# A fused attention and routing kernel: the third chunk's projections, the first DMAs and the order of the opening

## Chip, cores, metric

The kernel runs on one core of a Trainium2 chip. The metric is the device time of one execution in microseconds, the median over nine runs. Each core has TensorE (PE), VectorE (DVE), ScalarE (ACT), GpSimd (POOL) and SyncE (SP), all with instruction queues of their own, and 16 DMA engines that they share.

## What is computed

Attention with sketched features for 4 batches of 4 heads, 1088 positions of 32 numbers; its output, as 4352 rows of 128, is the input of 8 experts, weighted by 8 rounds of row and column scaling. S1 and S2 have 8 rows of 32; they come as 64-bit floats.

```python
def phi(x):
    a = np.einsum('rd,bhsd->bhsr', S1, x)
    b = np.einsum('rd,bhsd->bhsr', S2, x)
    return np.einsum('bhsi,bhsj->bhsij', a, b).reshape(*x.shape[:-1], r * r)
q_p, k_p = (phi(q), phi(k))
kv = np.einsum('bhsf,bhsd->bhfd', k_p, v)
z = np.sum(k_p, axis=2)
num = np.einsum('bhsf,bhfd->bhsd', q_p, kv)
den = np.einsum('bhsf,bhf->bhs', q_p, z)[..., None] + 1e-06
attn = num / den

x = np.ascontiguousarray(attn.transpose(0, 2, 1, 3)).reshape(B * S, H * D)
logits = x @ w_gate
P = np.exp(logits - logits.max())
for _ in range(8):
    P /= P.sum(1, keepdims=True) + 1e-09
    P /= P.sum(0, keepdims=True) + 1e-09
    P *= N / E
for e in range(E):
    out += P[:, e:e + 1] * (np.maximum(x @ w1[e], 0.0) @ w2[e])
```

## The kernel before

**Stages.** The opening computes batch 0's attention by itself. Then the experts' matmuls begin on what is ready of batch 0, with experts 0 and 1 unweighted, and the attention of batches 1 to 3 and the routing are woven in between their steps. From then on the experts 1 to 7 work on inputs weighted by the routing. The generator `steps()` (L1121) yields one step of expert work at a time: a matmul pair of the first layer (`first`, L920, matmul at L926, relu on ScalarE at L930) and, some steps later, pairs of the second layer (`into`, L1092, matmul at L1111). `fill(n)` (L1186) runs steps until n units of them are used, and carries the rest over. For groups of two tiles a unit is about two steps of 256 columns.

**Order.** Inside `manual_schedule` blocks TensorE and VectorE, in the first block ScalarE too, take the order of the program; elsewhere a planner may move instructions. `keep_in_program_order` holds a single instruction in place. Each engine runs its queue in order, so an instruction that waits holds up those behind it. SyncE issues most DMAs and waits in its queue too.

**The opening.** S1 is loaded by SyncE and S2 by ScalarE into one tile `raw`, each broadcast over the partitions (L101, L102). SyncE then loads keys, a first part of the queries and the values of batch 0, queries of batch 1, the rest of batch 0's queries, the gate's weights, expert 0's weights, and keys and values of batch 1 (L181 to L185, L292 to L295). 14 matmuls on ones (L114) run in the meantime. `projections()` (L258) turns 64-bit floats into 32-bit ones on VectorE (L34 to L46), transposes them (`st`, L262) and makes `wd` (L263), the projections of each head in its own partitions. `repeated()` (L267) makes on GpSimd, from `st`, `wq` (two heads in 64 partitions), `wdq` and `wz` (L280: one head in its partitions, zeros in the others). Then come the turned keys (`transpose_k`, L307, L309), their projections (`keys_ab`, L319, L324, copied out by ScalarE), their products on VectorE (`keys_products`, L336) and sums over positions (`keys_sums`, L352). ScalarE copies these to `kvz` (`keys_kept`, L367).

**Queries of batch 0** go in three chunks of positions, 0 to 512, 512 to 800 and 800 to 1088. `query_products(c)` projects them, ScalarE copies one factor to `ph` (L391), and `multiply` (L396, VectorE) multiplies it by the other, which stays in PSUM. `fractions(c, m)` (L404) makes numerators (m = 0) and denominators (m = 1), and `divide(c)` (L407 to L422, VectorE) writes `xT`, the experts' input. In `query_products` the chunks 0 and 1 use row tiles: two matmuls of 64 input partitions and 128 output columns run side by side (L381). Chunk 2 uses column tiles with all 128 input partitions and the weights `wz` (L387), one pair of heads at a time, in four groups of two.

**PSUM.** `bank()` gives one of four rotating banks; the others carry the tags s0 to s3, used by `query_products` of chunks 0 and 1, by `fractions` of chunks 1 and 2 (s2, s3) and by the experts' sums (`DIRECT` group: s0, s1).

**Batch 1's queries** go another way: `transpose_q(1)` (L302), `queries_ab(1)` (L438, copied by ScalarE at L441), then through DRAM (`qa`, `qb`, stored by SyncE and GpSimd, L445 and L449; read back by `repeat_a` and `repeat_b`, L455 and L458).

**Expert steps.** `step(c)` of `two` (L938) takes the four combinations of two blocks f of hidden units and two tiles t of positions in the order f = c // 2, t = c % 2 (L939, L940), so a block's second step already needs the second tile.

**Weights for three-tile groups.** `sums_of_four` (L226) makes 16 sums of weight blocks on GpSimd (L242) and stores them to DRAM by SyncE (L246) for later groups. `weigh` (L690) multiplies inputs by routing weights on GpSimd. `weigh_kept` (L706, called at L1148) weights the kept outputs of the early experts, one block into an expert at q = 0.

Of the kernel before, what the change touches and what calls it, by code (L numbers as in the profile page):

```python
# [50 lines left out]
def kernel(  # L51
# [12 lines left out]
    nc = tc.nc  # L64
# [29 lines left out]
    def bank():  # L94
        return aps.tile([P, 512], F32, tag="a", name="a")
# [2 lines left out]

    words = mybir.dt.size(S1.dtype) // 4
    raw = consts.tile([P, 2, words * D], U32, name="raw")  # L100
    for n, (s, queue) in enumerate(((S1, nc.sync), (S2, nc.scalar))):  # L101
        queue.dma_start(out=raw[:, n], in_=s.bitcast(U32).unsqueeze(0).to_broadcast([P // R, R, words * D]))  # L102

    def starts(tile_, c0, blocks):

# [120 lines left out]
    def sums_of_four(e, w2):  # L226

        ws = pools[0].tile([P, len(FORMS), FO // 4, H2], F32, tag="ws4", name="ws4")
        if e in stored_four:
            nc.sync.dma_start(out=ws, in_=stored_four[e])  # L230
            return ws

        def blocks(bs):
            b = w2[:, bs[0][1]::4, H2 * bs[0][0]:H2 * (bs[0][0] + 1)].unsqueeze(1)
            if len(bs) == 1:
                return b
            step = (bs[1][1] - bs[0][1]) * DM + (bs[1][0] - bs[0][0]) * H2
            return AP(tensor=b.tensor, offset=b.offset, ap=[b.ap[0], [step, 2], *b.ap[2:]])

        c = 0  # L240
        for ns, x, y, off in FOURS:
            tc.keep_in_program_order(nc.gpsimd.tensor_tensor(ws[:, c:c + len(ns)], blocks(x), blocks(y),  # L242
                                                             op=Alu.subtract if off else Alu.add))
            c += len(ns)
        stored_four[e] = dram.tile([P, len(FORMS), FO // 4, H2], F32, name=f"ws4{e}")
        nc.sync.dma_start(out=stored_four[e], in_=ws)  # L246
        return ws

    wd = consts.tile([P, 2, H, R], F32, name="wd")
    wq = consts.tile([P, 2, 2, R, R], F32, name="wq")

    wz = wk.tile([P, H, W9], F32, tag="xt", name="xt", bufs=1).rearrange("p h n -> p (h n)")[:, 0:2 * H * R * R]
    wz = wz.rearrange("p (n h i j) -> p n h i j", n=2, h=H, i=R)
    wdq = consts.tile([P, 2, H * R], F32, name="wdq")

    def projections():  # L258
        flat = raw.rearrange("p n d -> p (n d)")
        s12 = f64_to_f32(nc, consts, flat, (P, 2 * D)) if words == 2 else flat.bitcast(F32)  # L260
        st = consts.tile([P, 2, 32], F32, name="st")
        nc.vector.transpose(out=st.rearrange("p n r -> p (n r)"), in_=s12)  # L262
        nc.vector.tensor_tensor(wd, st[:, :, 0:R].unsqueeze(2).to_broadcast([P, 2, H, R]),  # L263
                                own.unsqueeze(1).unsqueeze(3).to_broadcast([P, 2, H, R]), op=Alu.mult)
        return st

    def repeated(st):  # L267
        def repeat(out, column):
            one = column.unsqueeze(2).to_broadcast([P, R, R])
            nc.gpsimd.tensor_tensor(out[:, 0], st[:, 0, 0:R].unsqueeze(2).to_broadcast([P, R, R]), one, op=Alu.mult)  # L270
            nc.gpsimd.tensor_tensor(out[:, 1], st[:, 1, 0:R].unsqueeze(1).to_broadcast([P, R, R]), one, op=Alu.mult)

        for s in range(2):
            repeat(wq[:, :, s], half[:, s:s + 1])


        nc.gpsimd.tensor_copy(wdq[:, 0], wd[:, 0].rearrange("p h r -> p (h r)"))
        nc.gpsimd.tensor_copy(wdq[:, 1].rearrange("p (r h) -> p r h", h=H), wd[:, 1].rearrange("p h r -> p r h"))
        for h in range(H):
            repeat(wz[:, :, h], own[:, h:h + 1])  # L280

    wdf = wd.rearrange("p n h r -> p (n h r)")
    wqf = wq.rearrange("p n h i j -> p n (h i j)")
# [84 lines left out]

    chunks = ((0, 512), (512, 800), (800, S))

    def query_products(c, i=None):


        lo, hi = chunks[c]
        n = hi - lo
        if c < 2:
            banks = [[mps.tile([P, 512], F32, tag=f"s{2 * i + m}", name="s") for m in range(2)] for i in range(2)]
            for m in range(2):
                for i in range(2):
                    sl = slice(64 * i, 64 * (i + 1))  # L380
                    nc.tensor.matmul(banks[i][m][:, 0:n], wqf[sl, m, :], qT[sl, lo:hi], start=True, stop=True,  # L381
                                     tile_position=(64 * i, 0))
        else:
            banks = {i: [bank(), bank()]}
            for m in range(2):
                for s in range(2):
                    nc.tensor.matmul(banks[i][m][64 * s:64 * (s + 1), 0:n],  # L387
                                     wz[:, m, 2 * i + s].rearrange("p i j -> p (i j)"), qT[:, lo:hi],
                                     start=True, stop=True, tile_position=(0, 64 * s))
        for j in range(2) if c < 2 else (i,):  # L390
            nc.scalar.copy(phs[0][:, j, lo:hi], banks[j][0][:, 0:n])  # L391
            queries[0, c, j] = banks[j][1][:, 0:n]

    def multiply(c, i):
        lo, hi = chunks[c]
# [8 lines left out]
            nc.tensor.matmul(t[64 * i:64 * (i + 1), 0:n], kvz[:, m, i].rearrange("p h d -> p (h d)"),  # L404
                             phs[0][:, i, lo:hi], start=True, stop=True, tile_position=(0, 64 * i))

    def divide(c):  # L407


        lo, hi = chunks[c]  # L410
        n = hi - lo
        nb = n // 32
        pn, pd = (queries.pop((0, c, "pn", m)) for m in range(2))
        rd = wk.tile([P, 512], F32, tag="rd", name="rd")
        nc.vector.transpose(out=rd[:, 0:n], in_=pd[:, 0:n])
        rc = wk.tile([P, 16], F32, tag="rc", name="rc")[:, 0:nb]
        nc.vector.tensor_scalar_add(rc, rd[:, 0:n].rearrange("p (b r) -> p b r", r=32)[:, :, 0], 1e-6)
        nc.vector.reciprocal(rc, rc)
        rd = wk.tile([P, 512], F32, tag="rd", name="rd")
        nc.vector.transpose(out=rd[:, 0:n].rearrange("p (b r) -> p b r", r=32),  # L420
                            in_=rc.unsqueeze(2).to_broadcast([P, nb, 32]))
        nc.vector.tensor_tensor(xT[:, lo:hi], pn[:, 0:n], rd[:, 0:n], op=Alu.mult)  # L422

# [508 lines left out]
    def two(k):  # L932

        j, q = blocks[k]
        n = groups[items[j][0]][1]
        h, ts, (later_h, earlier_h, t13) = hs[k] = room_of(k)

        def step(c):  # L938
            f, t = 2 * q + c // 2, c % 2  # L939
            first(k, f, t * n, (t + 1) * n, h[c], k % 2)  # L940

        def less(out, a, b):
            nc.vector.tensor_tensor(out, a, b, op=Alu.subtract)  # L943
# [177 lines left out]
    def steps():  # L1121

        todo, sums_at, t = {}, {}, 0
        for k in range(len(blocks) + 5):
# [5 lines left out]
            if k < len(blocks):  # L1130
# [11 lines left out]
                if q == 1 and j + 1 < first_weighted and not direct_of(j + 1) and loaded_w[j + 1][2] is None:  # L1142
                    w1, w2, _ = loaded_w[j + 1]
                    w = w1, w2, sums_of_two(items[j + 1][1], w2)
                    loaded_w.update({i: w for i in loaded_w if items[i][1] == items[j + 1][1]})
                if q == 0:
                    if weighted and 1 <= es.index(e) <= es[0] + 1:
                        weigh_kept(g, es.index(e) - 1)  # L1148
                if k == len(blocks) - HELD:
                    kept_to_sums(g)  # L1150
                m, step, sums_ = (four if tiles == 3 else two)(k)
# [34 lines left out]
    def fill(n):  # L1186
        owed[0] += n
        while owed[0] > 0.25:
            owed[0] -= next(work)

    with tc.manual_schedule(engines={engines.DVE, engines.PE, engines.Activation}):
        st = projections()
        repeated(st)
        halves = ((0, NT // 2), (NT // 2, NT))
        transpose_k(0, halves)
        keys_ab(0, halves)
        transpose_q(0, *chunks[0])
# [12 lines left out]
        query_products(1)  # L1210
        repeat_a(1)
        repeat_b(1)
        divide(0)
        load_q(2)
    with tc.manual_schedule(engines={engines.DVE, engines.PE}):
        for i in range(2):
            multiply(1, i)
        transpose_k(1)
        load_k(2)
        fill(1.25)  # L1220
        fractions(1, 1)
# [12 lines left out]
        multiply(2, 1)  # L1234
        fill(0.75)
        fractions(2, 1)
        fractions(2, 0)
        keys_products(1, 2)
# [46 lines left out]
```

## Time and profile before

| | us |
|---|---|
| median of 9 runs | 920.16 |
| lowest and highest | 919.76, 921.38 |
| the profiled execution | 919.77 |
| its span, first to last instruction | 918.0 |
| TensorE busy | 910.9 |
| VectorE busy | 683.7 |
| ScalarE busy | 421.2 |
| GpSimd busy | 208.0 |

The profile is of one execution. Busy is the time in which at least one instruction of an engine ran; matmuls are pipelined, so a busy TensorE is not one at its peak. The granted clock of TensorE was 0.999 of full speed over the span. Times in all views count from the span's start. A row of the chain gives start, duration, engine, tile and line, and how many instruction records it joins; each float32 matmul of a pair shows as one or two records. A row of the waits gives who waited for whom: total, times and the longest.

### The profile page before, as it was taken

Reading aid. Unit: us, or ns where it says so; the run is one execution under the profiler, and the core shown is the slowest. Engines: PE = TensorE matmul, PEld = TensorE weight load, DVE = VectorE, ACT = ScalarE, POOL = GpSimd, SP = SyncE. Lnnn points to the kernel's source line nnn. Section 1 sums busy time; section 2 is a strip of 40 time slices with the busy share of each in tenths; the row PEclk is TensorE's granted clock in tenths of the full one; section 3 lists DMA queues with packets and bytes.
Section 4 is the critical chain, followed back from the end, with each engine's and each line's share of the span. In section 5 each row is a group of like instructions: output and inputs, shape, how many; then the busy total and the mean of one; then the engine's idle time right before and its main releaser. Section 6 shows DMA issues by size and latency. Waiting matters only on the chain.

```text
span 918.0 us, 18917 instructions
## 1 busy us (share of the span) xinstructions
PE 910.9 (99%) x7450; PEld 593.9 (65%) x7450; DVE 683.7 (74%) x1173; ACT 421.2 (46%) x915; POOL 208.0 (23%) x220
## 2 busy tenths in 40 slices
PE   9999999999999999999999999999999999999997
PEld 6877544466666666666666666666666655556886
DVE  8678699888876798666976666956567977758665
ACT  3355555554444454444544444544445444445443
POOL 5121100175545421201210010110100233311120
PEclk9999999999999999999999999999999999999999
DMA  9994100213544535534364343464334465553650
GB/s 259 307 276 155 54 1 1 70 64 131 151 150 133 189 118 173 166 110 150 114 185 134 119 141 112 134 186 127 133 121 167 128 171 178 179 166 93 173 155 13
DMA packets 91305, 128.15 MB, mean 140 GB/s; under 512 B 25392, under 2 KB 69504, under 8 KB 86480
## 3 DMA queue, kind: packets, MB, share of 16 engines
q1 hardware_dynamic: 88384, 121.42, 42.5%
q0 software_dynamic: 1600, 5.36, 2.0%
q8 instruction: 58, 0.95, 0.4%
q10 hardware_dynamic: 1232, 0.16, 0.1%
q14 instruction: 31, 0.25, 0.1%
HBM read 107.88 MB, written 19.05 MB: 138 GB/s over the span
## 4 chain that ended last, share of the span: by engine, by line
PE 97%; DVE 2%; DMA 0%; issue 0%; ACT 0%; DVEq 0%
PE a L926 56%; PE s L1111 38%; PE a L352 1%; PE a L474 1%; PE a L319 0%; DVE hb L943 0%; PE s L381 0%; PE a L438 0%; DMA raw<-in_S_dram 0%; PE s L404 0%; PE a L508 0%; PE a L387 0%; PE a L404 0%; DVE cs L614 0%; DVE rs L608 0%
## 5 line engine op out<-in xcount | busy, mean ns | idle before, releaser
L926 PE MATMUL a<-xe,w 128*64 128x256 f32 (+1 forms) x2560 | 663.2, 470 | 0.0
L926 PEld LDWEIGHTS a<-xe,w 128*64 128x64 f32 x2560 | 300.6, 137 | 105.8 <-issue 1.6
L1111 PE MATMUL s<-hb,ws 128*64 128x256 f32 (+3 forms) x1312 | 314.0, 395 | 0.2 <-DVE hb L943 0.2
L930 ACT ACTIVATE hb<-a 128x256 f32<-128x256 f32 (+4 forms) x408 | 194.8, 480 | 242.0 <-PE a L926 208.2
L1111 PE MATMUL s<-hx,ws 128*64 128x256 f32 x1280 | 289.2, 379 | 0.0
L930 ACT ACTIVATE hx<-a 128x256 f32<-128x256 f32 (+1 forms) x360 | 167.2, 465 | 213.7 <-PE a L926 195.9
L990 DVE TENSOR_TENSOR hb<-hb 128x512 f32<-128x512 f32 (+1 forms) x204 | 137.1, 682 | 98.1 <-ACT hb L930 94.0
L1111 PEld LDWEIGHTS s<-hb,ws 128*64 128x64 f32 x1312 | 148.7, 137 | 77.7 <-issue 26.1
L990 DVE TENSOR_TENSOR hx<-hx 128x512 f32<-128x512 f32 (+1 forms) x204 | 149.7, 744 | 65.8 <-ACT hx L930 60.6
L690 POOL TENSOR_TENSOR xe<-xT,xe 128x768 f32<-128x768 f32 (+2 forms) x41 | 81.2, 1981 | 483.4 <-DMA xe<-pT 382.0
L1111 PEld LDWEIGHTS s<-hx,ws 128*64 128x64 f32 x1280 | 145.7, 137 | 62.5 <-issue 13.5
L1111 PE MATMUL s<-hb,w 128*64 128x256 f32 (+3 forms) x536 | 129.0, 408 | 0.0
L926 PE MATMUL a<-xT,w 128*64 128x416 f32 (+3 forms) x512 | 120.2, 462 | 0.0
L1111 PE MATMUL s<-hx,w 128*64 128x256 f32 x384 | 90.4, 379 | 0.0
L943 DVE TENSOR_TENSOR hb<-hb 128x416 f32<-128x416 f32 (+7 forms) x84 | 60.2, 717 | 20.6 <-ACT hb L930 16.7
L1111 PEld LDWEIGHTS s<-hb,w 128*64 128x64 f32 x536 | 57.9, 137 | 23.4 <-issue 6.6
L926 PEld LDWEIGHTS a<-xT,w 128*64 128x64 f32 x512 | 50.1, 137 | 24.3 <-issue 15.3
L242 POOL TENSOR_TENSOR ws<-w 128x256 f32<-128x256 f32 (+1 forms) x70 | 61.4, 911 | 7.8 <-DMA w<-in_moe_w_dram 5.1
L943 DVE TENSOR_TENSOR hx<-hx 128x256 f32<-128x256 f32 (+1 forms) x65 | 39.7, 614 | 24.0 <-ACT hx L930 22.8
L1111 PEld LDWEIGHTS s<-hx,w 128*64 128x64 f32 x384 | 44.1, 137 | 11.4
L990 DVE TENSOR_TENSOR pqg<-hb 128x512 f32<-128x512 f32 x68 | 43.2, 676 | 0.0
L990 DVE TENSOR_TENSOR pqg<-hx 128x512 f32<-128x512 f32 x68 | 36.3, 574 | 0.0
(184 smaller groups left out, 485.9 us busy)
## 6 DMA issues: line engine op xcount, KB each, us to landing
w<-in_moe_w_dram SPq DMA_DIRECT2D x82, 512.0 KB, 5.5
ws<-ws SPq DMA_DIRECT2D x34, 1024.0 KB, 5.1
xe<-pT SPq DMA_DIRECT2D x34, 384.0 KB, 4.0
ws<-ws SPq DMA_DIRECT2D x12, 512.0 KB, 3.8
ph<-qa SPq DMA_DIRECT2D x12, 288.0 KB, 5.0
rb<-qb SPq DMA_DIRECT2D x3, 1152.0 KB, 7.4
pb<-pT SPq DMA_DIRECT2D x6, 384.0 KB, 7.5
kx<-in_k_dram SPq DMA_DIRECT2D x4, 544.0 KB, 4.0
```

What stands on the lines that cost most here:

```text
L242: tc.keep_in_program_order(nc.gpsimd.tensor_tensor(ws[:, c:c + len(ns)], blocks(x), blocks(y), op=Alu.subtract if off else Alu.add))
L352: nc.tensor.matmul(pv[64 * s:64 * (s + 1), i], kp[0:n, H * t + h].rearrange("p i j -> p (i j)"), vx[0:n, slots[h], t, :], start=(t == 0 an ...
L474: nc.tensor.matmul(pn[64 * s:64 * (s + 1), t, 2 * i:2 * i + 2].rearrange("p h d -> p (h d)"), ph[:, i, s, 64 * t:64 * (t + 1)], kvs[b % 2] ...
L690: tc.keep_in_program_order(nc.gpsimd.tensor_tensor(out, x, pb, op=Alu.mult))
L926: nc.tensor.matmul(ph[sl], loaded_w[j][0][:, P * f + H2 * s:P * f + H2 * (s + 1)], sources[j][:, lo:hi], start=True, stop=True, tile_posit ...
L930: nc.scalar.activation(out=out, in_=ph, func=Act.Relu)
L943: nc.vector.tensor_tensor(out, a, b, op=Alu.subtract)
L990: nc.vector.tensor_tensor(out if not isinstance(out, tuple) else places(*out), places(*a), places(*b) if isinstance(b, tuple) else b, op=A ...
L1111: nc.tensor.matmul(sums[g][i][H2 * s:H2 * (s + 1), n * place:n * (place + 1)], w, x, start=c == 1, stop=c == per, tile_position=(0, H2 * s))
```

## The change

It has seven parts.

1. S1 and S2 are both loaded on ScalarE's queue, so that the keys are SyncE's first DMA.
2. `wd` is made by GpSimd in place of VectorE; `wz` and its eight multiplies go.
3. `query_products(2)` has row tiles as chunks 0 and 1, both pairs of heads in one call. Its first factors go to rotating banks, its second ones to s2 and s3. The tags in chunks 0 and 1 are numbered by factor first.
4. Batch 1's queries are transposed ahead of chunk 0's multiplies and projected (`queries_ab(1)`) ahead of `fractions(0, ...)`. The first two `fill` calls become 2.2 and 0.4; the later ones are joined.
5. `divide(0)` works in two halves of 256 positions.
6. The first two expert blocks are interleaved: block 0 does the first tile of both, block 1 the second tile of both.
7. Six of the seven DRAM stores of the sums of four go to GpSimd's queue, and `weigh_kept` is called one block later (q = 1).

```diff
-    for n, (s, queue) in enumerate(((S1, nc.sync), (S2, nc.scalar))):
-        queue.dma_start(out=raw[:, n], in_=s.bitcast(U32).unsqueeze(0).to_broadcast([P // R, R, words * D]))
+    for n, s in enumerate((S1, S2)):
+        nc.scalar.dma_start(out=raw[:, n], in_=s.bitcast(U32).unsqueeze(0).to_broadcast([P // R, R, words * D]))
...
-        nc.sync.dma_start(out=stored_four[e], in_=ws)
+        if e == 1:
+            nc.sync.dma_start(out=stored_four[e], in_=ws)
+        else:
+            tc.keep_in_program_order(nc.gpsimd.dma_start(out=stored_four[e], in_=ws))
...
-        nc.vector.tensor_tensor(wd, st[:, :, 0:R].unsqueeze(2).to_broadcast([P, 2, H, R]),
+        nc.gpsimd.tensor_tensor(wd, st[:, :, 0:R].unsqueeze(2).to_broadcast([P, 2, H, R]),
                                 own.unsqueeze(1).unsqueeze(3).to_broadcast([P, 2, H, R]), op=Alu.mult)
...
-        for h in range(H):
-            repeat(wz[:, :, h], own[:, h:h + 1])
...
-    def query_products(c, i=None):
+    def query_products(c):
         lo, hi = chunks[c]
         n = hi - lo
-        if c < 2:
-            banks = [[mps.tile([P, 512], F32, tag=f"s{2 * i + m}", name="s") for m in range(2)] for i in range(2)]
...
-        else:
-            banks = {i: [bank(), bank()]}
-            for m in range(2):
-                for s in range(2):
-                    nc.tensor.matmul(banks[i][m][64 * s:64 * (s + 1), 0:n],
-                                     wz[:, m, 2 * i + s].rearrange("p i j -> p (i j)"), qT[:, lo:hi],
-                                     start=True, stop=True, tile_position=(0, 64 * s))
...
+        banks = [[bank() if c == 2 and m == 0 else mps.tile([P, 512], F32, tag=f"s{2 * m + i}", name="s")
+                  for m in range(2)] for i in range(2)]
+        for m in range(2):
+            for i in range(2):
+                sl = slice(64 * i, 64 * (i + 1))
+                nc.tensor.matmul(banks[i][m][:, 0:n], wqf[sl, m, :], qT[sl, lo:hi], start=True, stop=True,
+                                 tile_position=(64 * i, 0))
...
-    def divide(c):
+    def divide(c, parts=1):
...
-        n = hi - lo
+        n = (hi - lo) // parts
...
+        for i in range(0, hi - lo, n):
+            rd = wk.tile([P, 512], F32, tag="rd", name="rd")
+            nc.vector.transpose(out=rd[:, 0:n], in_=pd[:, i:i + n])
...
         def step(c):
-            f, t = 2 * q + c // 2, c % 2
-            first(k, f, t * n, (t + 1) * n, h[c], k % 2)
+            b, f, t = k, c // 2, c % 2
+            if k < 2:
+
+                b, f, t = c // 2, c % 2, k
+            first(b, 2 * blocks[b][1] + f, t * n, (t + 1) * n, room_of(b)[0][2 * f + t], b % 2)
...
-                if q == 0:
-                    if weighted and 1 <= es.index(e) <= es[0] + 1:
-                        weigh_kept(g, es.index(e) - 1)
+                if q == 1 and weighted and 1 <= es.index(e) <= es[0] + 1:
+                    weigh_kept(g, es.index(e) - 1)
...
         keys_sums(0)
+        transpose_q(1)
         for i in range(2):
             multiply(0, i)
         keys_kept(0)
-        transpose_q(1)
         transpose_q(0, chunks[0][1])
+        queries_ab(1)
         fractions(0, 1)
-        queries_ab(1)
         fractions(0, 0)
...
-        divide(0)
+        divide(0, 2)
...
-        fill(1.25)
+        fill(2.2)
         fractions(1, 1)
         fractions(1, 0)
-        fill(0.75)
+        fill(0.4)
         divide(1)
         keys_ab(1)
         fill(0.75)
-        query_products(2, 0)
+        query_products(2)
         keys_products(1, 0)
         fill(0.75)
-        query_products(2, 1)
-        multiply(2, 0)
+        for i in range(2):
+            multiply(2, i)
         keys_products(1, 1)
-        fill(0.75)
-        multiply(2, 1)
-        fill(0.75)
+        fill(1.5)
         fractions(2, 1)
         fractions(2, 0)
```

More of the change, by code (lines that the diff above doesn't have):

```diff
@@ L252 @@
     wq = consts.tile([P, 2, 2, R, R], F32, name="wq")
-    wz = wk.tile([P, H, W9], F32, tag="xt", name="xt", bufs=1).rearrange("p h n -> p (h n)")[:, 0:2 * H * R * R]
-    wz = wz.rearrange("p (n h i j) -> p n h i j", n=2, h=H, i=R)
     wdq = consts.tile([P, 2, H * R], F32, name="wdq")
@@ L369 @@
     chunks = ((0, 512), (512, 800), (800, S))
-    def query_products(c, i=None):
+    def query_products(c):
         lo, hi = chunks[c]
         n = hi - lo
-        if c < 2:
-            banks = [[mps.tile([P, 512], F32, tag=f"s{2 * i + m}", name="s") for m in range(2)] for i in range(2)]
-            for m in range(2):
[L379 to L382, printed above, removed]
-        else:
-            banks = {i: [bank(), bank()]}
-            for m in range(2):
-                for s in range(2):
-                    nc.tensor.matmul(banks[i][m][64 * s:64 * (s + 1), 0:n],
-                                     wz[:, m, 2 * i + s].rearrange("p i j -> p (i j)"), qT[:, lo:hi],
-                                     start=True, stop=True, tile_position=(0, 64 * s))
-        for j in range(2) if c < 2 else (i,):
-            nc.scalar.copy(phs[0][:, j, lo:hi], banks[j][0][:, 0:n])
-            queries[0, c, j] = banks[j][1][:, 0:n]
+        banks = [[bank() if c == 2 and m == 0 else mps.tile([P, 512], F32, tag=f"s{2 * m + i}", name="s")
[6 more added lines that the diff above has]
+        for i in range(2):
+            nc.scalar.copy(phs[0][:, i, lo:hi], banks[i][0][:, 0:n])
+            queries[0, c, i] = banks[i][1][:, 0:n]
     def multiply(c, i):
@@ L405, in fractions @@
                              phs[0][:, i, lo:hi], start=True, stop=True, tile_position=(0, 64 * i))
-    def divide(c):
+    def divide(c, parts=1):
         lo, hi = chunks[c]
-        n = hi - lo
+        n = (hi - lo) // parts
         nb = n // 32
         pn, pd = (queries.pop((0, c, "pn", m)) for m in range(2))
[L414 to L422, printed above, removed]
+        for i in range(0, hi - lo, n):
+            rd = wk.tile([P, 512], F32, tag="rd", name="rd")
+            nc.vector.transpose(out=rd[:, 0:n], in_=pd[:, i:i + n])
+            rc = wk.tile([P, 16], F32, tag="rc", name="rc")[:, 0:nb]
+            nc.vector.tensor_scalar_add(rc, rd[:, 0:n].rearrange("p (b r) -> p b r", r=32)[:, :, 0], 1e-6)
+            nc.vector.reciprocal(rc, rc)
+            rd = wk.tile([P, 512], F32, tag="rd", name="rd")
+            nc.vector.transpose(out=rd[:, 0:n].rearrange("p (b r) -> p b r", r=32),
+                                in_=rc.unsqueeze(2).to_broadcast([P, nb, 32]))
+            nc.vector.tensor_tensor(xT[:, lo + i:lo + i + n], pn[:, i:i + n], rd[:, 0:n], op=Alu.mult)
     def queries_ab(b):
@@ L1226 @@
         fill(0.75)
-        query_products(2, 0)
+        query_products(2)
         keys_products(1, 0)
         fill(0.75)
-        query_products(2, 1)
-        multiply(2, 0)
+        for i in range(2):
+            multiply(2, i)
         keys_products(1, 1)
-        fill(0.75)
-        multiply(2, 1)
-        fill(0.75)
+        fill(1.5)
         fractions(2, 1)
```

## The prediction

> **What bounds the kernel now.** First the busy shares, then the list of TensorE's waits, then the chain that ended last.
>
> ```profile
> PE 910.9 (99%) x7450; PEld 593.9 (65%) x7450; DVE 683.7 (74%) x1173; ACT 421.2 (46%) x915; POOL 208.0 (23%) x220
> ```
>
> ```profile
> PE a L114 <- POOL own L116: 1.0, 1, 1.0
> PE a L404 <- ACT kvz L367: 0.6, 1, 0.6
> PE a L319 <- DVE kT L307: 0.3, 1, 0.3
> PE s L1111 <- DVE hb L943: 0.2, 1, 0.2
> ```
>
> TensorE never rests: 7.1 us of 918.0 are idle, and the named waits are 2.1 us, all but 0.2 before 13 us. The rest of the change's reach is work that TensorE need not do, and 14 warm-up matmuls (1.00 to 6.25) that only fill the wait for the first weights. So the opening's chain decides:
>
> ```profile
> 0.75 2.55 DMA raw<-in_S_dram
> ...
> 5.51 0.35 DVE wd L263
> 5.87 0.63 DVE kT L307
> 6.50 0.04 issue
> 6.54 1.28 PE a L319 x32
> ...
> 12.37 0.26 ACT kvz L367
> 12.63 0.01 issue
> 12.64 0.27 ACT kvz L367
> 12.91 0.04 issue
> 12.96 1.08 PE a L404 x4
> 14.04 0.97 PE a L438 x12
> 15.01 0.86 PE a L404 x4
> 15.87 1.17 PE s L381 x8
> 17.04 1.01 PE a L926 x8
> 18.05 1.15 PE s L404 x8
> ...
> 21.55 0.97 PE a L387 x8
> ...
> 22.95 0.97 PE a L387 x8
> ```
>
> S1 and S2 land, VectorE unpacks them, makes wd and turns the keys, then TensorE starts; it stops once more, for ScalarE's kvz copies (12.35 to 12.96), and from 13 us to the end it is the chain itself.
>
> **1. The start: +0.34.** The raw tile is whole at 3.30 (0.75 + 2.55). The trace's landings put ScalarE's half at 2.94 and SyncE's at 3.29. Now S2 is second on ScalarE's queue: the issue took 0.66 there, and SyncE's second DMA began 0.76 after its first, so S2 starts near 1.45; with the 2.19 that ScalarE's half needed it would land at 3.65 alone. That is the lower bound. But SyncE's first DMA is now kx, 544 KB, in flight at the same time. kx lands at 5.50 today, issued at 1.51; issued at 0.75 it lands near 4.75, and if S2's 128 packets (0.40 for ScalarE's half, 2.15 to 2.55) come behind it, S2 lands near 5.15. Neither end is shown. Nearest are the two halves themselves: issued together, ScalarE's packets all ran first and SyncE's from 2.6 on, so one queue can hold up another; yet kx began slowly, with 15 of 128 packets and the DMA engines 38% busy at the end of 3.0 to 3.4, which leaves room. I take 4.0, a quarter of the way: +0.70.
>
> [...]
>
> wd moves to GpSimd: VectorE loses 0.36 (5.51 to 5.87) ahead of the turns of the keys. GpSimd makes it in 0.29 (wq's multiply has the same size) inside the first turn's 0.63. Its four wq multiplies end 0.3 later, at 7.11 on the old clock, before their use at 7.95. Without that cover up to 0.3 would come back. Start: +0.70 − 0.36 = +0.34. kx then lands early and is not the limit while S2 comes after some 2.6.
>
> **2. The kvz wait: −0.61.** In the changed order TensorE does batch 1's query projections (six matmuls, 0.97) right after the key sums (end 12.35). Their turned input must be there: VectorE turns it (1.30) before the two multiplies, 10.56 to 11.86. The multiplies follow to 13.13, and fractions(0) can start at 13.35. VectorE covers this by 0.2; if it slipped, the wait would be back under another name.
>
> **3. The third chunk: −0.62.** Two L387 groups, 2 x 0.97 = 1.94, become one of four row-tile matmuls over 288 columns, the very form of L381 at 15.87: 1.17. A group of 4 passes over 288 columns is 0.97 by L387, so that row holds 0.20 more, and the L926 group behind it 1.01 against the usual 0.86. I count both: 1.17 + 0.15 = 1.32. If the excess was waiting only, the saving is 0.97.
> [...]
>
> **4. Two small waits: −0.40.** fractions(0) took 1.08 after its stop against 0.86 the second time; fractions(1) took 1.15 against 0.97. TensorE now comes to neither straight from a stop or from two steps (four steps stand between).
>
> **5. New waits: +0.9.** divide(0) is cut in halves. By the 288-column rows (0.48, 0.29, 0.25, 0.59, 0.46 from start to start, 2.07) a half of 256 columns costs 1.8, so VectorE spends 3.6 where it spent 2.75 (14.11 to 16.86). It starts at 14.5 (1.15 after fractions(0), as before), half one ends at 16.25; TensorE is through with query_products(1) at 13.35 + 1.71 + 1.17 = 16.23: wait 0.1. Four steps of 0.43 bring it to 18.05. In the changed VectorE order the three first pieces of half two and a turn stand among the multiplies of chunk 1: 16.25 + 0.9 + 0.41 + 0.45 + 0.41 = 18.4, and fractions(1) waits 0.4. Half two ends 18.85, the turn of batch 1's keys (1.45) 20.3; TensorE arrives at 19.9: 0.3. divide(1) ends 22.4, and the third chunk's second pair now writes banks that it reads; TensorE arrives at 22.3: 0.1. Together 0.9. Bounds: nothing if VectorE's rows overlap better, 1.5 if its start slips by 0.6 more. What stands behind VectorE then is the key products and divide(1), which the filling steps (12 in place of 11 before batch 1's key sums, 28.29) cover.
>
> **6. Nothing.** Eight zero-padded multiplies leave GpSimd (7.10 to 11.29); nobody waits for the engine until 15.74. Six 1 MB stores move from SyncE to GpSimd, behind the sums that they store and ahead of the next xe multiply: its other DMA issues took 0.52 to 0.67, so some 4 us over 130 us, while GpSimd idles 6 to 9 of every 20 us there and TensorE waits for no xe. SyncE's queue then no longer holds the xe loads behind a wait for the sums. weigh_kept runs a block later; its result is used at a group's end. Uncovered, these could cost the 2 us of one xe multiply.
> [...]
> The later order slides by a step; the one late wait, 0.2 near 160 us, may go or grow to some 0.5.
>
> **Sum.** 0.34 − 0.61 − 0.62 − 0.40 + 0.9 = −0.39. The profiled execution took 919.77 (span 918.0 and 1.77 around it): 919.38. It lies 0.39 under the median of the nine, 920.16, so I forecast 919.8 for the median. 0.2% is 1.84 us (918.32 to 922.00), about what a measurement of this kernel tells from no change.
>
> **Rivals.** (B) The whole gain: S2 lands at 3.65 (−0.35), no excess in the row tiles (−0.35), no new waits (−0.9): 919.8 − 1.6 = 918.2. For: VectorE idles 0.47 + 0.28 + 0.40 in 14 to 18.4. Against: the halves cost it 0.85 more.
> (C) Slower: S2 behind kx, landing 5.15, is 1.15 more: 919.8 + 1.15 = 920.9. The point from which this decides is a landing at 4.4 (4.0 + 0.39): later than that the kernel is slower than before. For: SyncE's half waited for ScalarE's. (D) The same mechanism further on: S2 shares every engine with the query and value loads too (v's first quarter lands at 7.16) and is whole only at 6.5: 919.8 + 2.5 = 922.3. Against: 128 packets of 256 bytes are little beside these.
> (E) It does not do what it says: kvz's wait only changes its name to VectorE's; then −0.61 is missing: 920.4.
>
> **Chances.** Forecast with E 0.48, B 0.26, C 0.17, D 0.09. Of B I put 0.22 beyond 918.32. So faster 0.22, same 0.69, slower 0.09. The range runs from B, 918.2, to midway between C and D, 921.6.
>
> **What would show it.** The first unpacking instruction: at 4.0, or 3.65, or 5.15. The first key projection (L319) 2.88 after that landing, where it is 3.24 now. No wait of L404 for kvz. One group of row-tile matmuls near 22 us, 1.0 or 1.2 long. Waits of TensorE for VectorE near 18.4 and 20.2. The total work ahead of the key sums at 28 us: one step more at the same time. A wait of TensorE after 30 us over 0.5, above all for xe near 200 us, would make the prediction wrong, and so would a landing beyond 5.2.

## The result, and the profile after

| | before | after |
|---|---|---|
| median, us | 920.12 (29 runs) | 924.25 (9 runs) |
| lowest and highest | 919.71, 921.43 | 922.62, 924.35 |
| the profiled execution | 919.77 | 922.43 |
| its span | 918.0 | 920.7 |
| start of the first projection | 6.54 | 9.05 |

The ratio is 1.0038, 95% interval 1.0030 to 1.0046: slower by 0.4%, above the forecast range (918.2 to 921.6). For the late start the mechanism was the third rival's, D (S2 shares the DMA engines with query and value loads too), to which the prediction gave 0.09. What was lost after the start was in no rival.

The busy shares and TensorE's waits of the changed kernel:

```profile
PE 910.5 (99%) x7442; PEld 532.2 (58%) x7442; DVE 689.8 (75%) x1177; ACT 420.9 (46%) x915; POOL 212.4 (23%) x219
```

```profile
PE a L318 <- DVE kT L306: 3.1, 1, 3.1
PE a L114 <- POOL own L116: 1.0, 1, 1.0
PE s L1107 <- DVE hb L939: 0.4, 1, 0.4
PE s L1107 <- DVE hb L986: 0.4, 1, 0.4
```

TensorE's work fell by 0.4, and the wait for the copies `kvz` is gone, as planned. But the wait for the first turned keys grew from 0.3 to 3.1, and the wait on a line-939 subtraction (L943 before) from 0.2 to 0.4; the one on L986 is new. The chain says why the first is so long:

```profile
0.74 0.66 ACTq L102
...
1.44 4.77 DMA raw<-in_S_dram
...
8.31 0.60 DVE kT L306
...
9.05 1.19 PE a L318 x32
...
10.37 1.99 PE s L380 x8
12.36 2.39 PE a L351 x72
14.75 1.13 PE a L431 x12
15.87 1.72 PE a L396 x8
17.59 1.17 PE s L380 x8
18.76 0.05 issue
18.81 1.95 PE a L919 x16
20.76 1.02 PE s L396 x8
```

The second of ScalarE's two S loads was issued at 1.44 and the tile `raw` was whole only at 6.20, against 3.30 before. From there the opening runs in one piece; its longest idle moment up to the second fractions is 0.05 before the first expert step (18.76).

**Where the 2.7 us went.** Both kernels have 768 relu instructions of expert steps. The n-th of one is matched with the n-th of the other; where TensorE has then done the same work in both, the difference of their starts is how far the changed kernel is behind. In the two profiled executions:

| up to | behind, us | change |
|---|---|---|
| first projection (9.05) | 2.51 | +2.51 |
| 36 to 72 us | 1.45 | −1.06 |
| 82 us | 2.18 | +0.73 |
| 203 us | 2.29 | +0.11 |
| 222 us | 2.91 | +0.62 |
| the last relu | 2.76 | −0.15 |

The middle parts of the change gained 1.06; a late start, a loss between 72 and 82 us and another near 214 took 3.86. That explains the profiled execution (2.66 longer), not the median (4.13 longer): of the ten executions that list a clock, three had a mean TensorE clock of 0.999 and took 922.43 to 922.84, seven had 0.997 or 0.998 and took 923.73 to 924.35. The experiments take up each of these.

**Why S came so late.** DMA packets of the changed kernel, from 1.5 to 3.4 us and then from 3.4 to 5.5 (number, MB, share of 16 engines; q1 is SyncE's queue, q10 ScalarE's):

```profile
DMA packets 110, 0.48 MB, mean 252 GB/s; under 512 B 0, under 2 KB 0, under 8 KB 110
...
q1 hardware_dynamic: 110, 0.48, 82.4%
```

```profile
DMA packets 730, 0.66 MB, mean 312 GB/s; under 512 B 341, under 2 KB 584, under 8 KB 730
...
q1 hardware_dynamic: 442, 0.59, 82.5%
q10 hardware_dynamic: 288, 0.07, 14.4%
```

In the first window only the keys move: 110 packets, all above 2 KB (4352 B each in the records), and none from ScalarE's queue, although both queues issued at 0.74. S1 and S2 are 256 packets of 256 B; all lie in the second window, 3.49 to 5.38, among packets of the queries (from 3.6) and the values (from 4.4). Before, S2's packets ran from 2.19 to 2.58 and S1's from 2.67 to 2.94, with the keys behind them. Both loads suffered. ScalarE's first load is in the changed kernel the same in size, queue and time of issue as its only one before. Before, its packets began at 2.19 and it landed at 2.94; now the first 128 of ScalarE's S packets run from 3.49 to 4.12 and it landed at 4.57. The second 128 run from 4.31 to 5.38, and that load landed at 6.20.

In the second window packets of both queues ran, 442 of SyncE's and 288 of ScalarE's. In the first no S packet ran in 1.9 us of key packets, and the trace doesn't tell whether S was already there to be picked.

### The profile page after: what moved, and what is told of

It reads as the page before. It is cut to its first block, busy times and chain, and to the rows that moved or that the text cites. A ratio compares the mean times of both kernels' runs of the same rounds, so it can differ in the third digit from the quotient of the medians.

```text
span 920.7 us, 18903 instructions
## 1 busy us (share of the span) xinstructions
PE 910.5 (99%) x7442; PEld 532.2 (58%) x7442; DVE 689.8 (75%) x1177; ACT 420.9 (46%) x915; POOL 212.4 (23%) x219
## 4 chain that ended last, share of the span: by engine, by line
PE 91%; DVE 6%; ACT 1%; issue 1%; DMA 1%; ACTq 0%; DVEq 0%
PE a L919 47%; PE s L1107 41%; DVE hb L939 1%; PE a L351 1%; DVE hb L986 1%; DMA raw<-in_S_dram 1%; PE a L467 0%; DVE kept L743 0%; PE s L380 0%; PE a L318 0%; PE a L431 0%; DVE rs L601 0%; ACT hb L923 0%; DVE p L604 0%; DVE w L746 0%
## 5 line engine op out<-in xcount | busy, mean ns | idle before, releaser
L919 PE MATMUL a<-xe,w 128*64 128x256 f32 (+1 forms) x2560 | 519.6, 470 | 0.0
L919 PEld LDWEIGHTS a<-xe,w 128*64 128x64 f32 x2560 | 202.1, 137 | 88.0 <-issue 1.6
L1107 PE MATMUL s<-hb,ws 128*64 128x256 f32 (+3 forms) x1312 | 232.9, 395 | 1.0 <-DVE hb L939 0.4
L986 DVE TENSOR_TENSOR hb<-hb 128x512 f32<-128x512 f32 (+1 forms) x204 | 137.6, 684 | 98.7 <-ACT hb L923 94.2
L1107 PE MATMUL s<-hx,ws 128*64 128x256 f32 x1280 | 206.8, 379 | 0.0
L986 DVE TENSOR_TENSOR hx<-hx 128x512 f32<-128x512 f32 (+1 forms) x204 | 153.5, 764 | 58.1 <-ACT hx L923 53.0
L1107 PEld LDWEIGHTS s<-hb,ws 128*64 128x64 f32 x1312 | 106.4, 137 | 117.3 <-issue 86.3
L1107 PEld LDWEIGHTS s<-hx,ws 128*64 128x64 f32 x1280 | 103.3, 137 | 100.1 <-issue 73.1
L919 PE MATMUL a<-xT,w 128*64 128x416 f32 (+3 forms) x512 | 120.5, 463 | 0.2
L1107 PE MATMUL s<-hb,w 128*64 128x256 f32 (+3 forms) x536 | 107.6, 408 | 0.0
L1107 PE MATMUL s<-hx,w 128*64 128x256 f32 x384 | 68.6, 379 | 0.0
L919 PEld LDWEIGHTS a<-xT,w 128*64 128x64 f32 x512 | 49.0, 137 | 26.1 <-issue 16.4
L1107 PEld LDWEIGHTS s<-hb,w 128*64 128x64 f32 x536 | 46.6, 137 | 23.2 <-issue 7.0
L986 DVE TENSOR_TENSOR pqg<-hb 128x512 f32<-128x512 f32 x68 | 42.3, 663 | 0.0
L1107 PEld LDWEIGHTS s<-hx,w 128*64 128x64 f32 x384 | 33.5, 137 | 11.6
L986 DVE TENSOR_TENSOR pqg<-hx 128x512 f32<-128x512 f32 x68 | 38.0, 597 | 0.0
```

The lines of the kernel that those rows point to most:

```text
L919: nc.tensor.matmul(ph[sl], loaded_w[j][0][:, P * f + H2 * s:P * f + H2 * (s + 1)], sources[j][:, lo:hi], start=True, stop=True, tile_posit ...
L986: nc.vector.tensor_tensor(out if not isinstance(out, tuple) else places(*out), places(*a), places(*b) if isinstance(b, tuple) else b, op=A ...
L1107: nc.tensor.matmul(sums[g][i][H2 * s:H2 * (s + 1), n * place:n * (place + 1)], w, x, start=c == 1, stop=c == per, tile_position=(0, H2 * s))
```

## The experiments

The kernel before, run beside them, had medians of 920.22 (runs 1 to 4), 920.33 (5, 6, 8, 9) and 920.51 (7). Single executions of the kernel before spread over 919.5 to 922.2, and the intervals of most ratios reach 0.8 us to either side. Where less is at stake, the matched traces are all there is, and each of them is of one execution.

### 1. The S loads back on two queues

The changed kernel without part 1:

```diff
-    for n, s in enumerate((S1, S2)):
-        nc.scalar.dma_start(out=raw[:, n], in_=s.bitcast(U32)...)
+    for n, (s, queue) in enumerate(((S1, nc.sync), (S2, nc.scalar))):
+        queue.dma_start(out=raw[:, n], in_=s.bitcast(U32)...)
```

> The changed kernel with S1 on SyncE's queue and S2 on ScalarE's again, all else as changed. Theory: the loads on one queue cost the start 2.9 us (raw whole at 6.20 in place of 3.30) and all of the slower runs, whose mean clock of 0.997 comes from the 3.1 us in which TensorE idles before its first projection. Then raw is whole near 3.3, TensorE starts near 6.2 (the keys land at 5.5), every run has a clock of 0.999, the span is 920.7 - 2.8 = 917.9 and the median 919.7 to 920.0. Rival: the loss lies in the body (the collisions after 60 us) and the start matters little; then the median stays over 922.

Measured: 920.73 (920.09 to 921.27, 11 runs), ratio 1.0005 (0.9996 to 1.0014). So part 1 cost 3.5 of the 4.1 us. The median didn't come to the time expected, for two reasons. The keys, second on SyncE again, now set the start:

```profile
1.51 4.71 DMA kx<-in_k_dram
...
6.25 0.72 DVE kT L306
...
7.11 1.19 PE a L318 x32
```

They landed at 6.22 here, at 5.50 in the profile of before: the start is 0.57 late, though VectorE has lost `wd`. And the two later losses are there in full: ahead of before by 0.49 at 70 us, behind by 0.24 at 87 and by 1.25 at 219.

### 2. The S loads alone

The kernel before with nothing but part 1 (the diff above, reversed, on the kernel before).

> The kernel before with S1 and S2 both on ScalarE's queue, nothing else. Theory: raw is whole near 6.2, TensorE's first projection begins 3.24 later, at 9.4 in place of 6.54, so the span is 918.0 + 2.9 = 920.9; runs with a clock of 0.997 are 1.8 us longer, and the median is 922.5 to 924.5, slower by 0.25% or more from this edit alone. Rival (the other edits carry the loss): within 0.2% of 920.1.

Measured: 923.98 (923.72 to 925.04, 5 runs), ratio 1.0042 (1.0030 to 1.0055). Part 1 alone makes the whole slowdown; the rest of the change, taken together, comes out near nothing. In the trace the first projection starts at 9.29, 2.75 late, yet from the first expert step on the kernel is 4.27 behind, and it ends 4.06 behind. The other 1.5 are in the stretches of TensorE's clock (the stretch, its length, busy us and instructions of PE, PEld, DVE, ACT and POOL, the granted clock, the DMA share and GB/s):

```profile
6.61:10.02 3.41, 1.17 (x24) 0.93 (x25) 3.20 (x14) 0.00 (x0) 1.77 (x8) 1.00 0.96 274
10.02:13.43 3.41, 3.41 (x24) 2.10 (x25) 3.37 (x4) 1.11 (x4) 3.41 (x6) 0.50 1.02 308
13.43:16.85 3.42, 3.17 (x76) 2.26 (x72) 2.54 (x4) 1.01 (x3) 0.62 (x3) 1.00 1.04 276
```

The clock's records of all the profiles within TensorE's work are 3.41, 907.95, 911.36 and 914.77 us long: 1, 266, 267 and 268 times 3.413. A stretch here is one such length, counted from the start of a record. TensorE was busy in 1.17 of the first one above, having waited from 7.05 to 9.29 for the first turned keys; the next stretch ran at half clock, which by estimate costs up to 3.41 / 2 = 1.7 of matmul time. All five executions had a mean clock of 0.996 to 0.998. A mean of 0.998 alone is no proof: every profile has a half-clock record at its end, after TensorE's last matmul (from 916.28 of 918.0 us in that of before), and single executions of before list 0.998 at 919.86 us. None of the 68 executions of before that list a clock is lower, though; the changed kernel has 0.997 in four of its ten.

### 3. Warm-up matmuls across the wait

The changed kernel with 28 warm-up matmuls in place of 14, so that TensorE is busy until the keys come:

```diff
-    for _ in range(14):
+    for _ in range(28):
```

> The changed kernel with 28 warm-up matmuls in place of 14, so that TensorE is busy until about 9.0. Theory: the lower clock of most runs comes from the idle 5.98 to 9.05; with it filled all runs have 0.999 and lie at 922.4 to 922.9, while the changed kernel's lay at 922.6 or near 924.2. The span of the profiled run stays at 920.7. Rival: the clock varies for another reason, and the runs stay in two groups.

Measured: 923.64 (922.72 to 924.38, 5 runs), ratio 1.0035 (1.0023 to 1.0048). The clock did what was expected: 0.999 or 1.000 in every execution. The time was expected at 922.4 to 922.9 and came down by 0.6 only, less than the intervals tell apart: executions at full clock went up to 924.38, with spans of 920.9 to 922.0. The warm-ups themselves end at 9.16, so the start is no earlier, and the profiled execution lost 0.89 near 214 us in place of 0.62. So the link from the idle stretch to the clock is shown here and in run 2; its price in the time of the changed kernel is shown by neither to better than some 0.5 to 1.5 us.

### 4. The stores back on SyncE

The changed kernel without part 7:

```diff
-        if e == 1:
-            nc.sync.dma_start(out=stored_four[e], in_=ws)
-        else:
-            tc.keep_in_program_order(nc.gpsimd.dma_start(out=stored_four[e], in_=ws))
+        nc.sync.dma_start(out=stored_four[e], in_=ws)
...
-                if q == 1 and weighted and 1 <= es.index(e) <= es[0] + 1:
+                if q == 0 and weighted and 1 <= es.index(e) <= es[0] + 1:
```

> The changed kernel with all stores of the sums of four on SyncE again and the kept outputs weighted at q = 0 as before. Theory: with the stores on GpSimd the xe load came earlier, its multiply ran at 212.1 beside a VectorE add that then took 2.71 us, and TensorE lost 0.62 there; with them back this step in the lag behind the kernel before (2.29 to 2.92 us at 214 us) is gone, the span is 920.1, the median 0.6 lower. Rival: the loss there is chance of the phase and stays; then the span is 920.7.

Measured: 921.78 (921.52 to 924.33, 10 runs), ratio 1.0019 (1.0010 to 1.0029). The six executions at a clock of 0.999 or more took 921.52 to 921.82, against 922.43 to 922.84 of the changed kernel at that clock: part 7 costs 0.9. The median fell by more, 2.5, because six of ten executions were at that clock in place of three of ten; nothing here shows that part 7 has to do with that. (The other four are at 0.997 to 0.998. The profiled one is one of them: S landed at 7.22 in it, TensorE was busy for 0.50 of the stretch from 6.86, and the next one was at half clock.) In the matched traces no time is lost near 214 us. What was lost there in the changed kernel is seen in its order of time, first GpSimd and VectorE, then TensorE:

```profile
210.80 3.69 DVE L986 TENSOR_TENSOR hb<-hb 128x512 f32<-128x512 f32 x2
...
211.49 0.60 POOL L250 DMA_DIRECT2D ws<-ws  x1 [0.30 <-POOL ws L242]
...
212.11 1.82 POOL L683 TENSOR_TENSOR xe<-xT,xe 128x768 f32<-128x768 f32 x1
...
214.54 0.65 PE L1107 MATMUL s<-hb,ws 128*64 128x256 f32 x4 [0.39 <-DVE hb L986]
```

and in the kernel before at the same work, VectorE's rows and then GpSimd's:

```profile
208.78 1.41 DVE L990 TENSOR_TENSOR hb<-hb 128x512 f32<-128x512 f32 x2
...
214.17 2.91 DVE L990 TENSOR_TENSOR hx<-hx 128x512 f32<-128x512 f32 x2
```

```profile
206.81 1.50 POOL L242 TENSOR_TENSOR ws<-w 128x128 f32<-128x128 f32 x2
214.62 1.90 POOL L690 TENSOR_TENSOR xe<-xT,xe 128x768 f32<-128x768 f32 x1 [6.32 <-DMA xe<-pT]
```

Two adds that take 1.41 take 3.69 when GpSimd's multiply of 1.82 falls among them. Before, GpSimd waited 6.32 for its input, because SyncE could issue that load only at 208.76, behind the store that waits for the sums; then the multiply met a pair of adds (2.91) that nobody waited for. With the stores off its queue, SyncE issues the load near 206, though the kernel is 2.3 behind, and at equal work the multiply runs 4.8 us earlier (212.11 − 2.3 against 214.62), beside adds that TensorE does wait for. The run undoes both halves of part 7, but the later `weigh_kept` isn't in this: its first multiply on GpSimd starts at 229.99 in the changed kernel (235.31 before), after the loss.

The pair of adds grew by 2.28, a little more than the multiply's 1.82. In run 1 the same pair took 3.55, with a multiply of 1.82 beside it too; in run 4's trace, where GpSimd is idle at that point, it takes 1.41. The traces show that the two go together, not by what means.

### 5. Parts 1 and 7 both undone

The changed kernel with the diffs of runs 1 and 4 together.

> The changed kernel with both the S loads and the stores (with the kept outputs' weighting) as before, the rest as changed. Theory: the two losses add, so this is the kernel with the loads back (920.7) less the collision at 211 us (0.9): 919.8, not slower than the kernel before. In the trace no wait of TensorE between 205 and 220 us. Rival: the collision only moves; then it stays near 920.7.

Measured: 920.25 (919.57 to 920.83, 11 runs), ratio 0.9998 (0.9990 to 1.0007). No different from before; the median can't tell the 919.8 that was expected from the rival's 920.7. The keys landed later still:

```profile
1.51 5.16 DMA kx<-in_k_dram
...
7.55 1.19 PE a L315 x32
```

From a start 1.01 late it was level with before (−0.04) at 70 us, so the opening gained 1.05, about what it did in the changed kernel; by 81 us it was 0.68 behind. That loss has nothing to do with the loads or the stores. Near 214 us nothing is lost: 0.80 behind at 180 us and at 260.

### 6. The third chunk's row tiles alone

The kernel before with part 3 alone: the new `query_products`, whose diff the change shows, and no `wz`.

```diff
-        query_products(2, 0)
+        query_products(2)
         keys_products(1, 0)
         fill(0.75)
-        query_products(2, 1)
         multiply(2, 0)
```

> The kernel before with row tiles for the third chunk alone (one call of four matmuls, no zero-padded weights). The prediction's term is 0.62 (1.94 down to 1.32), with 0.97 if the excess of the row-tile group is waiting alone. At equal work after 40 us the lead over the kernel before should be 0.6 to 1.0; the median 919.3 to 919.6 unless the start or a collision differs. [...]

Measured: 920.38 (919.23 to 921.20, 11 runs), ratio 0.9998 (0.9989 to 1.0007). The chain shows the group and what came of it:

```profile
21.46 0.89 PE a L377 x4
22.35 0.48 PE s L377 x4
22.83 1.88 PE a L915 x16
...
33.37 0.39 ACT hb L919
...
33.93 0.90 PE a L463 x24
```

The group takes 0.89 + 0.48 = 1.37 where two took 1.94, and the steps behind it run slower, 1.88 for 16. Lead over before: 0.09 at the first step, 0.50 from 25 to 32 us, so 0.41 for the edit; at 33.9 TensorE waits 0.2 for ScalarE (`PE a L463 <- ACT hb L919: 0.2, 1, 0.2` in the list of waits) and the lead is down to 0.05; between 62 and 71 us the order differs from before's and 0.86 is lost. The edit is right where it stands, and is not worth anything at the end.

### 7. The earlier queries alone

The kernel before with only the order of part 4:

```diff
         keys_sums(0)
+        transpose_q(1)
         for i in range(2):
             multiply(0, i)
         keys_kept(0)
-        transpose_q(1)
         transpose_q(0, chunks[0][1])
-        fractions(0, 1)
         queries_ab(1)
+        fractions(0, 1)
         fractions(0, 0)
```

> The kernel before with the order of part 4 alone: batch 1's queries are turned ahead of the two multiplies and projected ahead of fractions(0). The loads, the third chunk, the whole division and the fills stay. Prediction's step 2: TensorE's wait of 0.61 for the copies kvz goes, VectorE's two multiplies end 1.3 later (near 13.1) and fractions(0) starts near 13.3, so the division, not cut in halves, ends near 17.5 in place of 16.86. TensorE reaches the first expert step some 0.6 sooner than before, that is before xT is there: a wait of 0.3 to 0.6 at the first step takes the place of the one removed. Theory (the wait only moves, and the halves of part 5 were needed to keep the gain): lead of 0.6 at 15 us, given back by 19 us, 920.0 to 920.3. Rival (VectorE has room, the gain stays): a lead of 0.6 at 30 us and 919.6. Second rival: the lead slides the later order and is lost by 80 us, as in the runs with one step more ahead of the second pass.

Measured: 920.52 (919.74 to 920.96, 11 runs), ratio 0.9998 (0.9989 to 1.0007). TensorE's waits:

```profile
PE a L926 <- ACT ph L391: 0.9, 1, 0.9
PE s L1111 <- DVE hb L943: 0.2, 1, 0.2
```

The `kvz` wait of 0.6 is gone and one of 0.9 stands before the first step, which needs all of `xT`. (The list names ScalarE's copy of L391; that ended at 16.81. VectorE's division ended at 17.37, and TensorE went on at 17.47.) Start 0.43 late, because the warm-up matmuls ended only at 6.97 (the last section says why), and 0.49 behind at that step: the wait was renamed, as the prediction's rival E said. In the changed kernel, which has the halves of part 5, no such wait appears; that the halves are what keeps the gain wasn't tested apart.

### 8. One expert step less ahead of the second pass

Run 5's kernel with one expert step less before the third chunk's fractions, to test whether the loss between 72 and 82 us comes from the order having slid by a step:

```diff
-        fill(1.5)
+        fill(0.9)
         fractions(2, 1)
```

> As the kernel with both back, but with fill(0.9) in place of fill(1.5) after the third chunk, so that the expert steps stand to the later attention as before. Theory: the 0.7 us that are lost between 65 and 80 us (lag 1.46 to 2.18) come from one step too many, which puts VectorE's subtractions behind attention work; with it taken back this loss goes and the median is 919.1. Rival: the loss comes from something else in that stretch; then the time is that of the kernel with both back, 919.8.

Measured: 920.20 (919.42 to 920.99, 11 runs), ratio 0.9999 (0.9990 to 1.0007). In the traces the loss is gone: a lead over before of 0.16 at 70 us, of 0.16 at 80, of 0.35 at the end (a span of 917.6). It isn't the time of the start that does it: the six kernels with the changed order (the changed one and runs 1, 3, 4, 5 and 9) lose 0.7 to 0.8 there, though they come to 60 us between 0.5 ahead of before and 3.9 behind it. But 0.3 each went to two waits that run 5 didn't have:

```profile
PE a L464 <- ACT hb L920: 0.3, 1, 0.3
PE a L428 <- DVE kT L298: 0.3, 1, 0.3
```

The wait for `hb` is that of run 6, at 33.8, where a lead of 0.64 falls to 0.2; the one for `kT` is for batch 1's queries, which landed at 10.98 and are turned by 12.39, while TensorE is ready for them at 12.27. This is the shortest span of all profiles, and the kernel's median can't be told from before's.

### 9. Both S loads on SyncE, ahead of the keys

The changed kernel with S1 and S2 on one queue as in the change, but SyncE's, so that nothing else runs beside them (the diff below). If a second load on one queue is slow in itself, S stays late; if it was the competition, S comes early and the keys late.

```diff
-        nc.scalar.dma_start(out=raw[:, n], in_=s.bitcast(U32)...)
+        nc.sync.dma_start(out=raw[:, n], in_=s.bitcast(U32)...)
```

> The changed kernel with S1 and S2 both on SyncE's queue, ahead of the keys. Theory: S2 was late because kx's packets went first on the same 16 DMA engines, not because it is the second DMA on its queue. Then raw is whole by 3.7, the keys follow and land near 6, TensorE starts near 7, no run has a lowered clock, and the median is 920.5 to 921.5. Rival: the second of two such broadcasts on one queue is itself 2.5 us late; then raw is whole at 5.5 or later here too and the median stays near 923.

Measured: 921.52 (920.54 to 921.64, 10 runs), ratio 1.0010 (1.0001 to 1.0019), clock 0.999 or more throughout. VectorE's first row of the conversion and its first turn of the keys:

```profile
3.62 0.20 DVE L34 TENSOR_SCALAR mant<-raw 128x64 uint32<-128x64 uint32 x1 [1.88 <-DMA raw<-in_S_dram]
...
6.31 1.30 DVE L306 STREAM_TRANSPOSE kT<-kx 128x512 f32<-128x512 f32 x2 [0.67 <-DMA kx<-in_k_dram]
```

Two loads in a row on one queue were whole at 3.53, 0.23 later than on two queues. So a second load on a queue isn't slow in itself, and S behind none of the large loads is 2.67 us sooner than the 6.20 of the changed kernel. The run doesn't use ScalarE's queue for S; that this queue alone isn't slow is shown by its load of before, through at 2.94. What is left is the competition.

The median lies at the upper end of what was expected. The start was held by something else:

```profile
1.00 6.34 PE a L114 x28
7.33 1.08 PE a L318 x32
```

The first projection stood behind the last warm-up matmul, 0.79 later than before; and part 7's loss is in this trace too (0.47 behind at 211 us, 1.35 at 214).

## Why the prediction was wrong

**The step that failed is step 1.** It placed S2's landing at 4.0, a quarter of the way from 3.65 to 5.15; it came at 6.20, outside both bounds. The upper bound took the keys to be the only load in the way. In fact keys were sent until 3.85, with no packet of S before 3.49, and S then shared the engines with the queries and values, which SyncE had issued at 1.18 and 1.64, before ScalarE's second load was through. The prediction had this as its last rival (landing 6.5, time 922.3). Its choice went by "15 of 128 packets and the DMA engines 38% busy at the end of 3.0 to 3.4". That was misread. Of the 15 packets, these started from 3.0 to 3.2 and from 3.2 to 3.4:

```profile
q1 hardware_dynamic: 11, 0.05, 126.2%
...
q1 hardware_dynamic: 4, 0.02, 37.8%
```

The view counts a packet's time where the packet starts. The first eleven were long and ran on; counted where they run, packets took 99% of the engines' time from 3.2 to 3.4. The room that the choice went by wasn't there. The other half of step 1 was right: from landing to first projection 2.85, forecast 2.88.

**The half clock was in no step.** A late start was priced at the waiting alone. Run 2's trace shows that a stretch at half clock can follow, by estimate up to 1.7; that seven of the changed kernel's ten executions had one is argued from their lower mean clock and longer time, and from run 3.

**Step 2** (−0.61) was right, with a larger cover than forecast: VectorE's multiplies ended at 15.27, 0.6 ahead of the row at 15.87. Run 7 shows the gain lost where the division isn't halved. **Step 3**: 0.62 forecast, 0.41 at once in run 6, with the group itself 1.37. So the excess beside row tiles is there and a little larger than forecast; its cause no run shows. **Step 4** (−0.40): the rows of L396 are 1.72 where 1.08 and 0.86 stood and 1.02 where 1.15 stood, 0.35 less; the query projections ahead of them gave back 0.16 (1.13 for 0.97). **Step 5**: 0.9 of new waits forecast, 0.05 seen. VectorE's halves ran in time. So the opening, net of the start, gained 1.06 where the steps say 0.73: a sum whose terms erred in both directions.

**Step 6, costed at nothing, cost 0.6 to 0.9.** The cover was named as GpSimd's idle time and TensorE waiting for no `xe`, and the price without cover as the 2 us of one multiply. Both were true, and beside the point: an earlier multiply isn't late itself, it makes VectorE late (3.69 for 1.41). The last sentence of the step, that the late wait near 160 us might grow to 0.5, was right (0.43).

**What no step had** is the loss between 72 and 82 us. In run 8 it is gone with one expert step less, so it belongs to how the order has slid against the second pass's attention work. In the rows, two second-layer matmuls wait for a subtraction at 71.9 that stands behind VectorE's attention work; that and the gap of 0.11 at 79.1 account for less than half. How the rest comes about wasn't settled.

Rival D had the start's mechanism but not the time. Its 922.3 is a median, 2 short of 924.25. For the profiled execution it comes to 919.38 + 2.5 = 921.9, against 922.43: S2's landing 0.3 too late, the opening's gain 0.3 too small, and nothing of the 1.3 lost after it. That it looks close is partly luck.

## What to carry to other kernels

A DMA that is small and wanted first is best kept ahead of large loads in time: here S was whole at 3.53 on the keys' own queue ahead of them (run 9), and at 6.20 on another queue beside them, when the queries and values issued behind the keys ran among its packets too. Where a change moves an engine's work earlier, ask not only whether that work is late but whose instructions it will now run beside: here a pair of adds went from 1.41 to 3.69. And a few tenths won in a woven opening are worth something only if the order behind it is looked at again; here gains of 0.4 to 1.0 in runs 5, 6 and 8 were lost in whole or in good part within some 60 us.

## What the runs showed of the hardware

- A wait of TensorE was followed by the half clock in run 2 and not in the profiled changed kernel, where it was longer (3.08 against 2.24). There, from 5.97 to 9.05, it lay across two stretches, and neither was followed by a half clock:

```profile
4.35:7.76 3.41, 1.62 (x14) 1.43 (x13) 1.42 (x10) 0.00 (x0) 0.00 (x0) 1.00 0.99 223
7.76:11.18 3.42, 2.11 (x38) 1.74 (x40) 3.35 (x8) 0.84 (x3) 1.89 (x8) 1.00 0.89 301
```

  TensorE was busy for 1.62 and 2.11 of them. The stretches that were followed by one had 1.17 (run 2) and 0.50 (run 4). That busy time is what decides, these four stretches suggest and don't prove.
- Ahead of the clock's records the warm-up matmuls ran more slowly. In run 9 the records begin at 7.20 (the column's 1.00 ahead of that is no record), in the changed kernel at 4.35. Two lengths of 3.41 in run 9 ahead of that, then the last one ahead of it in the changed kernel:

```profile
0.37:3.78 3.41, 2.78 (x13) 2.79 (x14) 1.02 (x5) 1.48 (x2) 2.29 (x26) 1.00 0.20 41
3.78:7.20 3.42, 3.42 (x17) 3.26 (x16) 2.64 (x14) 0.00 (x0) 1.48 (x6) 1.00 0.99 314
```

```profile
0.94:4.35 3.41, 3.35 (x15) 3.36 (x16) 0.79 (x3) 1.47 (x2) 2.01 (x23) 1.00 0.74 233
```

  A record of the warm-up matmuls, two for each, takes 0.20 to 0.22 in these rows (13 in 2.78, 17 in 3.42, 15 in 3.35) and 0.12 in the changed kernel's next one (14 in 1.62). That the clock was lower ahead of the records is an estimate from this pace. Behind the row with 2.78 busy the pace stayed, behind the one with 3.35 it rose.
  The 14 warm-ups ended at 5.97, 6.25 and 7.33 in the profiles of the change, of before and of run 9, where the clock's records begin at 4.35, 4.93 and 7.20. In runs 7, 8 and 9 the first projection stands right behind them (6.97, 6.77, 7.33), so there they, and neither S nor the keys, set the start.
- A load of 544 KB from the same place, issued at the same 1.51 or 1.52 behind an S load, landed at 5.50, 6.22 and 6.67 in the profiles of before and of runs 1 and 5, and at 5.39, 5.89 and 5.43 in those of runs 6, 7 and 8. That spread alone is as large as what the opening's edits could win.
